# Giving the values' PSUM bank back between runs of products, with the sums gathered in SBUF, and a new written order

## The chip, the cores and the metric

The kernel runs on one core of one Trainium2 chip. The metric is device time of one execution, in microseconds (us). Before the change it is 1624.57 us, the median of three runs (1624.36 to 1624.93). Five engines work side by side, each through its own list of instructions in a fixed order: TensorE (PE in the profile, with its weight loads as PEld), VectorE (DVE), ScalarE (ACT), GpSimd (POOL) and SyncE (SP), which here issues every DMA.

## The reference

All inputs are fp32. `x` is 2048 tokens by 512; attention has 32 heads of 16, and one shared key head and value head.

```
q = (x @ wq) as 32 heads of 16;  k = x @ wk;  v = x @ wv          # k, v: 2048 x 16
p = softmax(q k^T / 4)                                            # per head, 2048 x 2048
a = concat(p @ v) @ wo
b = (sigmoid(x @ w_gate) * (x @ w_up)) @ w_down                   # 512 -> 1792 -> 512
g = sigmoid(sum(x * gate_w))                                      # one number per token
out = g * a + (1 - g) * b
```

The factors on `wq` and `wk` make the scores large, so each row's maximum is taken before the exponential.

## The kernel before, in words

**Units of attention.** The tokens are cut in 4 blocks of 512 and the heads in 8 groups of 4. One block with one group is a unit `u`; there are 32. A unit needs three kinds of products on PE:

- `m` (line 1074): scores with the queries as rows. DVE reduces each 128x512 tile to its row maxima (line 1076). 64 tiles per unit.
- `s` (line 1083): the scores again, turned, with the maxima subtracted by extra rows of the product. ACT takes the exponential of each tile into an SBUF buffer `p` (line 1085). 64 tiles per unit.
- `V` (line 965, function `pv`): the values. One `V` takes the four `p` tiles of one chunk of 128 keys and multiplies them by `v_aug`, in which a row of ones makes the denominators too. A unit has 16 of them, and all 16 add into one PSUM bank; the four matmuls of a `V` go to four groups of 32 rows of that bank.

When a unit's sixteenth `V` is done, ACT copies the bank to the SBUF tile `ou` (line 973, `finish`), five DMAs take it on (lines 981 and 984), and the division and the output projection follow.

**The rest of PE's work** is `f` (line 1053): the matmuls of the gated MLP and of the output projection. Their results leave PSUM through ACT (`gate`, and `part` with "first" or "apart", line 1034) or DVE (`gated`, and `part` with "sum", lines 1063 and 1016). A token tile's first part is written to the tile `ba` by ACT with "first"; later parts are added to it by DVE with "sum", or set apart by ACT and added by GpSimd (line 1037).

**How PE is shared.** The contraction of `m`, `s` and `f` is 64 rows or fewer, so two of them run at a time, one in the upper and one in the lower half of the array. That is one step. A `V` uses all 128 rows, in four groups of 32 columns, so PE changes its tiling before a run of `V`s and again behind it. The first projections (`G` in the order) use the whole array too.

**Banks.** There are 8 PSUM banks. Each `m`, `s` and each group of `f` takes a free one and gives it back when ACT or DVE has read it. The values' bank is held from a unit's first `V` to the copy behind its sixteenth, so that 7 banks are left for the steps.

**What sets the order.** The string `ORDER` is read one character at a time by a planner (`State.step`). `V`, `G` and `T` (a transposition of maxima) stand for themselves; a hexadecimal digit is one step, whose two base-4 digits say what goes into each half (0 nothing, 1 `m`, 2 `s`, 3 `f`); `.` is a short wait. The planner keeps a clock for every engine, a time at which each bank and buffer comes free, and tasks for GpSimd with ranks. It emits the list of actions that the kernel issues, and that list is the fixed order of every engine. The planner's times are not seen by the chip: the engines wait on semaphores.

```
        self.acts.append(("part", h, j, i, "sum"))
        at = self.on("dve", at, SUM)
```

These two lines plan a "sum" on DVE; the time at which ACT has written the tile's "first" does not enter.

Of the kernel before, what the change touches and what calls it, by code (L numbers as in the profile page):

```python
# [18 lines left out]
P = 128  # L19
# [11 lines left out]
RAW, WB, DB, PB, HB, BA_BUFS = 2, 2, 4, 22, 6, 4  # L31
# [18 lines left out]
IN, OUT, VALUES, TURN = 52, 94, 371, 50  # L50
# [60 lines left out]
class State:  # L111

    def __init__(self):
# [3 lines left out]
        self.free, self.sum = [0] * 7 + [4100], None  # L117
        self.later, self.count = [], 0
# [21 lines left out]
        self.held, self.exps = 0, []  # L140
        self.loaded, self.stage_free, self.unit_ready, self.max_ready, self.q_ready = 0, 0, {}, {}, {}
# [60 lines left out]
    def run(self, t):  # L202
        self.tasks.remove(t)
        what, *args = t[3]
        if what == "w":
            wide = args[0][0] in "gu"
            cost = (not self.early(args[0])) * CAST_W + TWO_W if wide else (1 + (args[0][0] != "e")) * (CAST + TWO)
        else:
            cost = {"h": CAST + TWO, "add": TWO, "stack": CAST_W + 2 * TWO_W, "divide": CAST + 2 * TWO, "x": 2 * TWO,
                    "xf": 4 * TWO, "wq": TWO}[what]  # L210
# [60 lines left out]
    def event(self, what, args):  # L271
# [17 lines left out]
        elif what == "store":  # L289
            self.after(self.send(5, 136) + SAFE, "sums", *args)  # L290
# [131 lines left out]
    def gather(self, j, h, i, second, at):  # L422

        key = (j.b, j.i % NT)
        if key not in self.parts:
# [5 lines left out]
            return self.on("act", at, SCALED)  # L431
# [7 lines left out]
        at = self.on("dve", at, SUM)  # L439
# [61 lines left out]
    def can_v(self):  # L501
        return (self.first > GROUPS.index(("turn", NB - 1, 0)) and self.vp < NU * NC and bool(self.exps)
                and (self.vp % NC > 0 or min(self.free) <= self.now)
                and self.exps[0][0] == 4 and self.exps[0][1] <= self.now)

    def issue_v(self):
        u, c = divmod(self.vp, NC)
        if c == 0:
            self.sum = self.take()
        self.acts.append(("values", u, c, self.sum))  # L510
# [5 lines left out]
        if c == NC - 1 and u < NU - 1:  # L516
            self.acts.append(("finish", u, self.sum))
            at = self.on("act", self.now + LATE, COPY) + TAIL_A
            self.free[self.sum] = at + FREE
            self.after(at, "store", u)  # L520
# [76 lines left out]
    def step(self, code):  # L597


        self.tick()  # L600
        if code == ".":
# [25 lines left out]
    "GGGGGGGG555G555G5554GG555G555G55G555GG55G555G555GG555G555GT55.Gd7ffdb6fbdfe7bde7bf9fe7edbf6f9fe7fbde7bfdV696V559"  # L627
    "VVV6bdff79fef7fedb7ff9f6ffdef6fdf6fbdf7bd7VVV9e7ffdb7efdfb7edff6dbff7bf97ffed6ffbd7d.VT69V696V965VV9e7ffdb7efdfb"
    "7edff6f9ff7bf9f7fede7fd7d7VVVb9ef7df6fdbef6fdbf6f9f7bef9fe7fdb6fdbf7ed7V969V696V95aV696Va59V696Va59VT69V569VVe6b"
    "fdfb7ef9fe7bf9f7deVV6bd7ffedbef7bf9f7eef5.V965VVd6bfdb7ef9fe7bdeb7f9fffef6fdbf6f9fe7bdef7V969VVV6fbdef6fbdbf6fd7"  # L630
    "dVVV6fbdbf6fbf9fef6fbdef5f7d7VVVTbb7fffdef97fefedbf6ff9fe7bf9fe7ef9fe7d36V969VV696V596VV96fbfd7bf9fe7edbe7f9f7eb"
    "def7bdef6fdbb7efd7dVVV695VV6bbdff6fbdef6fbdbf6fbd7f9VVVTee7fffd6bfdfbef5V69bfff6fbdef6fbdbf5feVV6bbfdfe7bf9fe7ef"
    "9f7deV695VV6958VV79fe7edbf6fbde7bf9f6ffffedb7ef9f6fdb7edf7VV95aV696V596VV9eb7ff9fe7ef9fe7bf9fe7df6fdbVVVTeb7fffd"
    "6beff.9VV6f9ff7edbf7fedb7ff97effdef6fdfb79ff7edbV55aVV696V969V69fef7dbf6fbd7ef9ef7bf9f6fdeb7efdbf6f9f7d7eVVV969V"
    "696V969V696V9T6Vbe9ff7ef9fe7bf9fe7ef9f7d7VVV9ee7ff9fe7bf5febdV695VV6bedff6fbdbf6fd7df6VVd6bfdb7bf9fe7edbf6f9f7de"
    "bVV696Vb9fe7fed7f9VV6bf9ffe7ebdV69efff6fdb7Vb9ef7fed7f9VVTebefff7b5fefbefd7d7VVb9ef7fedbf6fbdef7d7d7VVbedbf7ef9f"
# [45 lines left out]
def tile_kernel(ctx, tc, x_in, wq, wkv, wo, wg, wu, wd, consts_in, out):  # L682
# [279 lines left out]
    def pv(u, c, ps):  # L962

        for j in range(4):
            nc.tensor.matmul(ps[32 * j:32 * j + 32, :], v_aug[:, c, :], PT.pop((u, c, j)),  # L965
                             start=c == 0, stop=c == NC - 1)

    SUMS = {}
# [213 lines left out]
```

## Time and profile before

| | |
|---|---|
| median of 3 runs | 1624.57 us (1624.36 to 1624.93) |
| profiled execution, its own time | 1625.31 us |
| its span, first to last instruction | 1623.5 us |
| PE busy | 1614.7 us (99%) |
| DVE busy | 1419.7 us (87%) |
| ACT busy | 1187.6 us (73%) |
| POOL busy | 773.8 us (48%) |
| mean clock granted to TensorE | 0.999 of full speed |

In the profile, a row names a line of the kernel, the engine, the operation, and the tiles as output<-inputs, with the number of instructions behind an x. Times are in us unless marked ns. A `V` shows as eight records of line 965, since each of its four fp32 matmuls leaves two. Matmuls are pipelined, so one record (about 0.4 us for a step's matmul) is longer than the distance to the next start; the distance between starts is what a matmul costs.

### The profile page before, as it was taken

What the parts mean: (1) busy time and instruction counts of PE and PEld (TensorE: products, weight loads), DVE (VectorE), ACT (ScalarE), POOL (GpSimd) and SP (SyncE); (2) the same over time, 40 slices, a digit from 0 to 9 for tenths busy, and PEclk for the clock granted to TensorE, in tenths of its full rate; (3) what the DMA queues carried; (4) which work ended last, traced back from release to release, by engine and by line L of the source; (5) the groups of instructions that cost most, each with busy time, mean ns of one, the idle gap of its engine ahead of it and who ended that gap; (6) DMA issues with size and microseconds to landing.
All of it is one profiled execution on the core that took longest, in us unless ns stands there. A gap on an engine that the chain in (4) does not pass through costs nothing.

```text
span 1623.5 us, 33536 instructions
## 1 busy us (share of the span) xinstructions
PE 1614.7 (99%) x12950; PEld 982.2 (60%) x12950; DVE 1419.7 (87%) x2422; ACT 1187.6 (73%) x2274; POOL 773.8 (48%) x598
## 2 busy tenths in 40 slices
PE   9999999999999999999999999999999999999998
PEld 7665566555666566655656556565566656566554
DVE  6999898999998989999998998888998999889842
ACT  4277777677777767777776877767877777777786
POOL 5344264457454534463726346435645454536152
PEclk9999999999999999999999999999999999999999
DMA  7311111024111211111412121102411121111011
GB/s 234 135 52 44 44 54 48 27 71 107 59 45 45 77 35 59 39 44 54 122 32 70 38 76 54 47 29 70 106 60 48 44 76 43 58 31 34 32 35 40
DMA packets 52371, 98.10 MB, mean 60 GB/s; under 512 B 17976, under 2 KB 19512, under 8 KB 51188
## 3 DMA queue, kind: packets, MB, share of 16 engines
q1 hardware_dynamic: 52212, 95.96, 19.2%
q8 instruction: 102, 1.67, 0.4%
q14 instruction: 57, 0.47, 0.1%
HBM read 74.05 MB, written 8.90 MB: 51 GB/s over the span
## 4 chain that ended last, share of the span: by engine, by line
PE 98%; ACT 1%; DVE 1%; DMA 0%; SPq 0%; issue 0%; DVEq 0%; ACTq 0%
PE bank L1053 31%; PE bank L965 30%; PE bank L1074 17%; PE bank L1083 16%; PE bank L819 3%; ACT p L1085 1%; DVE mx L1076 0%; DMA xf<-x_in 0%; PE bank L950 0%; DVE ba L1130 0%; DMA qs<-mt 0%; ACT x L737 0%; PE bank L889 0%; DVE ba L1016 0%; ACT ba L1034 0%
## 5 line engine op out<-in xcount | busy, mean ns | idle before, releaser
L1076 DVE TENSOR_REDUCE mx<-bank 128x1 f32<-128x512 f32 x2048 | 1285.7, 683 | 124.4 <-PE bank L1074 68.4
L1085 ACT ACTIVATE p<-bank 128x512 f32<-128x512 f32 x2048 | 1068.3, 621 | 334.8 <-PE bank L1083 162.2
L1083 PE MATMUL bank<-qs,ks 64*128 64x512 f32 x2048 | 748.4, 408 | 0.4 <-DVE ba L1016 0.3
L1074 PE MATMUL bank<-ks,qs 62*128 62x512 f32 x2048 | 709.7, 410 | 0.6 <-ACT q L911 0.3
L965 PE MATMUL bank<-p,v_aug 128*32 128x512 f32 x4096 | 502.3, 599 | 0.0
L1083 PEld LDWEIGHTS bank<-qs,ks 64*128 64x128 f32 x2048 | 356.4, 185 | 142.0 <-DVE mx L1076 54.7
L1074 PEld LDWEIGHTS bank<-ks,qs 62*128 62x128 f32 x2048 | 341.1, 184 | 160.1 <-DVE mx L1076 68.2
L1053 PE MATMUL bank<-wd,hl 64*128 64x512 f32 x1344 | 261.4, 394 | 0.0
L965 PEld LDWEIGHTS bank<-p,v_aug 128*32 128x32 f32 x4096 | 102.7, 108 | 226.8 <-issue 208.6
L1053 PE MATMUL bank<-xs,wg 64*128 64x512 f32 x672 | 210.6, 393 | 0.0
L1053 PE MATMUL bank<-x,wu 64*128 64x512 f32 x672 | 209.6, 392 | 0.0
L1053 PE MATMUL bank<-xs,wu 64*128 64x512 f32 x672 | 209.1, 393 | 0.0
L1053 PE MATMUL bank<-x,wg 64*128 64x512 f32 x672 | 206.8, 392 | 0.0
L1053 PEld LDWEIGHTS bank<-wd,hl 64*128 64x128 f32 x1344 | 182.0, 185 | 29.7 <-DVE mx L1076 6.7
L937 POOL TENSOR_TENSOR qs<-stage,qs 16x1024 fp32r<-16x1024 f32 x62 | 148.8, 2400 | 4.8
L1053 PEld LDWEIGHTS bank<-x,wu 64*128 64x128 f32 x672 | 118.3, 185 | 10.2 <-DVE mx L1076 0.8
L1053 PEld LDWEIGHTS bank<-xs,wu 64*128 64x128 f32 x672 | 117.4, 186 | 10.3 <-issue 2.5
L1053 PEld LDWEIGHTS bank<-xs,wg 64*128 64x128 f32 x672 | 118.4, 186 | 7.3
L1053 PEld LDWEIGHTS bank<-x,wg 64*128 64x128 f32 x672 | 116.9, 186 | 8.5 <-POOL wu L795 0.8
L794 POOL CAST wu<-ru 128x1024 fp32r<-128x1024 f32 x27 | 28.0, 1038 | 175.7 <-PE bank L1053 140.5
L1037 POOL TENSOR_TENSOR ba<-ba,pa_d 128x512 f32<-128x512 f32 x48 | 61.8, 1290 | 76.0 <-DVE ba L1016 46.1
L935 POOL CAST qs<-stage 128x1024 fp32r<-128x1024 f32 x31 | 32.2, 1039 | 131.2 <-PE bank L1083 90.6
(85 smaller groups left out, 1074.0 us busy)
## 6 DMA issues: line engine op xcount, KB each, us to landing
rg<-wg SPq DMA_DIRECT2D x28, 512.0 KB
ru<-wu SPq DMA_DIRECT2D x28, 512.0 KB
rd<-wd SPq DMA_DIRECT2D x28, 512.0 KB
stage<-qd SPq DMA_DIRECT2D x192, 64.0 KB
xs<-x SPq DMA_DIRECT2D x16, 512.0 KB
xf<-x_in SPq DMA_DIRECT2D x16, 256.0 KB
qd<-q SPq DMA_DIRECT2D x16, 256.0 KB
ra<-wo SPq DMA_DIRECT2D x8, 512.0 KB
```

The lines of the kernel that those rows point to most:

```text
L794: nc.gpsimd.tensor_copy(WS[item][:, 0, :], raw)
L819: nc.tensor.matmul(ps, w[:, p, part(kc)], X[b, kc][:, q, :], start=i == 0, stop=i == 3 * KC - 1)
L935: (nc.scalar.copy if u == 0 else e.tensor_copy)(qs, stage)
L937: e.tensor_tensor(qs[r], stage[r], f32(qs[r]), op=ALU.subtract)
L965: nc.tensor.matmul(ps[32 * j:32 * j + 32, :], v_aug[:, c, :], PT.pop((u, c, j)), start=c == 0, stop=c == NC - 1)
L1037: nc.gpsimd.tensor_tensor(BA[b, t], BA[b, t], PA.pop((b, t)), op=ALU.add)
L1053: nc.tensor.matmul(banks[i], l, r, start=at == 0, stop=at == j.n - 1)
L1074: nc.tensor.matmul(banks[i], qs_t[u % 3][r, pr, part(qt)], ks[r, kb * 512:(kb + 1) * 512], start=True, stop=True)
L1076: nc.vector.tensor_reduce(MX[u][:, pr, h, qt, kb:kb + 1], banks[i], axis=AX.X, op=ALU.max)
L1083: nc.tensor.matmul(banks[i], ks[r, part(c)], qs_t[u % 3][r, pr, :], start=True, stop=True)
L1085: nc.scalar.activation(p, banks[i], AF.Exp, scale=0.25)
```

## The change

1. **The bank is given back between runs.** A new character `C` in the order closes the values' bank: the `V` ahead of it ends its accumulation there, ACT copies the sums so far to one of two SBUF tiles (`sums_out`, which replaces `finish`), and the bank is free again. The next `V` takes a new bank and starts it afresh. The first closing of a unit leaves its sums in a tile `OU[n]`; each later one is copied to the other tile, and GpSimd adds it on (`sum_add`, a 128x512 fp32 addition, a task of rank 1). Behind the unit's last closing the sums are stored from `OU[n]`. The last unit is not closed; the kernel's end reads its bank as before.
2. **One `p` buffer fewer** (PB from 22 to 21), for the second `ou` tile.
3. **The planner's book-keeping:** a "sum" is planned no earlier than its tile's "first" (`first_at`), and a `T` counts 20 in place of 50 of the planner's units.
4. **A new order string.** Counted in both strings, with `C` left out of the count of runs:

| | before | after |
|---|---|---|
| `V` | 512 | 512 |
| `G`, `T` | 24, 32 | 24, 32 |
| steps (hexadecimal digits) | 4265 | 4259 |
| of these with one half empty | 30 | 18 |
| `.` | 10 | 13 |
| `C` | 0 | 99 |
| runs of `V` | 303 | 251 |
| runs of one, two, three `V` | 146, 105, 52 | 60, 121, 70 |
| runs of `G` followed by a step or `T` | 14 | 12 |

The numbers of `m`, `s` and `f` are the same in both (2048, 2048 and 4404). With the 31 units that are closed at their end there are 130 closings, where 31 copies were.

```diff
-RAW, WB, DB, PB, HB, BA_BUFS = 2, 2, 4, 22, 6, 4
+RAW, WB, DB, PB, HB, BA_BUFS = 2, 2, 4, 21, 6, 4
-IN, OUT, VALUES, TURN = 52, 94, 371, 50
+IN, OUT, VALUES, TURN = 52, 94, 371, 20
...
+        elif what == "sum_add":
+            u, i, n, last = args
+            self.ou_free[i] = at
+            if last:
+                self.after(at, "store", u, n)
...
-            return self.on("act", at, SCALED)
+            self.first_at[key] = self.on("act", at, SCALED)
+            return self.first_at[key]
...
-        at = self.on("dve", at, SUM)
+        at = self.on("dve", max(at, self.first_at[key]), SUM)
...
-        if c == 0:
+        new = self.sum is None
+        if new:
             self.sum = self.take()
...
+    def close(self, u, last):
+        self.acts[self.v_at] = (*self.acts[self.v_at][:4], True, self.sum)
+        i = self.ou_free.index(min(self.ou_free))
+        assert self.ou_free[i] <= self.now or last
+        self.acts.append(("sums_out", i, self.sum))
+        at = self.on("act", max(self.now + LATE, self.ou_free[i]), COPY) + TAIL_A
+        self.free[self.sum], self.sum, self.ou_free[i] = at + FREE, None, NEVER
+        if self.ou is not None:
+            self.task(1, at + SURE, "sum_add", u, i, self.ou, last)
+        elif last:
+            self.after(at, "store", u, i)
+        else:
+            self.ou = i
+        if last:
+            self.ou = None
...
+        if code == "C":
+            self.close(self.vp // NC, False)
...
-    def pv(u, c, ps):
+    def pv(u, c, new, last, ps):
...
-                             start=c == 0, stop=c == NC - 1)
+                             start=new, stop=last)
...
-        SUMS[u] = ap.tile([P, TB], F32, tag="ou", name=f"ou{u}", bufs=1)
-        nc.scalar.copy(SUMS[u], ps)
+    OU = [ap.tile([P, TB], F32, tag=f"ou{i}", name=f"ou{i}", bufs=1) for i in range(2)]
+    def sums_out(i, ps):
+        nc.scalar.copy(OU[i], ps)
+    def sum_add(_, i, n, last):
+        nc.gpsimd.tensor_tensor(OU[n], OU[n], OU[i], op=ALU.add)
```

More of the change, by code (lines that the diff above doesn't have):

```diff
@@ L208, in run @@
         else:
-            cost = {"h": CAST + TWO, "add": TWO, "stack": CAST_W + 2 * TWO_W, "divide": CAST + 2 * TWO, "x": 2 * TWO,
+            cost = {"h": CAST + TWO, "add": TWO, "sum_add": TWO, "stack": CAST_W + 2 * TWO_W, "divide": CAST + 2 * TWO, "x": 2 * TWO,
                     "xf": 4 * TWO, "wq": TWO}[what]
@@ L289, in event @@
         elif what == "store":
-            self.after(self.send(5, 136) + SAFE, "sums", *args)
+            u, i = args
+            self.ou_free[i] = self.send(5, 136)
+            self.after(self.ou_free[i] + SAFE, "sums", u)
         elif what == "sums":
@@ L502, in can_v @@
         return (self.first > GROUPS.index(("turn", NB - 1, 0)) and self.vp < NU * NC and bool(self.exps)
-                and (self.vp % NC > 0 or min(self.free) <= self.now)
+                and (self.sum is not None or min(self.free) <= self.now)
                 and self.exps[0][0] == 4 and self.exps[0][1] <= self.now)
@@ L507, in issue_v @@
         u, c = divmod(self.vp, NC)
-        if c == 0:
+        new = self.sum is None
+        if new:
             self.sum = self.take()
-        self.acts.append(("values", u, c, self.sum))
+        self.v_at = len(self.acts)
+        self.acts.append(("values", u, c, new, c == NC - 1, self.sum))
         self.now += VALUES
@@ L516, in issue_v @@
         if c == NC - 1 and u < NU - 1:
[L517 to L520, printed above, removed]
+            self.close(u, True)
+    def close(self, u, last):
[13 more added lines that the diff above has]
+            self.ou = None
     def can_t(self):
@@ L597, in step @@
     def step(self, code):
-        self.tick()
-        if code == ".":
+        if self.last != "C":
+            self.tick()
+        if code == "C":
+            self.close(self.vp // NC, False)
+        elif code == ".":
             self.now += 25
@@ L632 @@
[L632 to L636, printed above, removed]
@@ new lines @@
+    "ef9f6fbdef6f9fb7d7df5fVVV65VVC97edfbf6ff96fbdf6fbdef6f9fb7edbf6fbde7fbd7dVVC655VV965VVCb9f6ffde7bf9fTffee6ffdb7b"
+    "f9f6f9f6fdeb7efd7.VVV965VV9e6ffdf6fbdbf6f9fb7ed7bedbf7edbf6fdbe7bfd7dV696VVC965VVC97fedb7ef9fe7bdef6f9f7VVVC97fe"
+    "db7ef9fe7bdef6f9f7VVCTbf9fff79fe7edef6ff97VVC97defb7ef9f6fbde7bf5feVV965VV97f9fe7fedb7ef9f7ef9fe7bdef6f9fb7ef9f6"
+    "fbde7VV955VVVC6d7bfedbf6f9fe7dbef6ff9f6fbdb7ef9fe7bdef5f7VV9TaVVVC69fef7dbf6fbf97ef9f6fdeb7efdb7ef9f7ebd7fd7dVVV"
+    "696V965VV9e6ffdf6fbdb7dbe7bfdef6f9f7bedbf7ef9f6fd7d7VV969V696VCd6bbfd7ef9fe7bdef6f9fbVVC6T9VVVC69fef7dbf6fbde7bf"
@@ new lines @@
+    "9f6fdVVC69fef7dbf6fbde7bf9f6fdV696VV965VVd6bfdb7ef9fe7bdef6f9f7VVC9e6ffdf6fbdbf6f9f6f9fb7edbf7edbf6fbde7bfd7dVVV"
+    "696V596VVCTfbff9ff69f6ff9fe7edbf6f9fe7bf9f6fedf6fbd7.V969V696V95aV6a5VV969VV56fbfedbf6f9fe7bdef6fbdb7efdb7ef9fe7"
+    "bd7f5fdVVV696V9a6V969VVC6fdbf6fbdef6db7bf9f7eedbf7edbfTff6fbdff6d7VVV96aV596VVC96fdfb7ef9f6fbde7fb9fe7f9fe7edfb6"
+    "fdbfe7d7d7VVVdb6ff9fe7bdV696VV96aV969VC6fdbf6f9fe7ffbfdef7fbfed6fbd7..VV9TaVC6bdef7bdfe7bedb7d7fedbVVVC6bdef7f9f"
+    "e7bedb7def7dbVVC6bdef7bdfe79feb7d7fedbVVV6bdef7bdfe7bedb7edf6f1bVVVC6bdbf7edfbf6dfbf6bdfe79f7ef9ef7bf9f7edf6fdV6"
@@ new lines @@
+    "96V965VV9T5VVC69fbf7def6fbd7bedbf7ef9f6fdbe7bfdef6f9f7bdVV69eV569VVVC6dfb7bdef6f9f7bedbf7ef9f6fdbe7bfdef6f9f7d7d"
+    "VV696VV969VVC6dbf7bdef6fbdb7edbf6ff9e7bfdefb7edbfTff6fdVV695VVVC65ffbfdbe7bdfe7bdef6fbdb7ef9f6fbdef7bdef7dVV696V"
+    "C5bf9fe7bf9f6fedb7dfebVVV79fefef6f9fbe7dbf6f9feVVV695VVC69fbf7edfb7edbf6f9fe7fbff9ff6f9fe7ef9fe7dVVV6T9V695VVC6d"
+    "fb7bdef6fbdb7ef9f6ffffbf9f6fedbf6f9f7deVVV696VV9ff6db7bf9fe7ebdff69feVVC6bdbf7edfb7ebde7d7fbdeVVVC6bdbf7edfbf6bf"
+    "9ef6fdf6f9f7bf9f7f9eef7fde7dVVV6T9VVC6fdbf6f9f6f9f7bedbf7ef9f6fdbe7bfdef6f9f7d7dVV69aV655VVVdb6fbdb7ff96fedff6bd"
@@ new lines @@
+    "bf7edbf6f9fe7bf9f6fed7dVVVCa65VVC9f7bde7bf9fe7edb7ef9fe7dbef7bf9fe7edbfTff5cV695VVC6df6fbdbf6f9fe7bdef5fbVVVC65f"
+    "bfedbf6f9fe7bdef7beVVV969VV7edbf6f9fe7bfde7bf9f7fef9f7eef9f7ef9f6fdbV696V965VVV965VVC9f7ef9fe7bfTefbdef79e7bfdef"
+    "6f9fb7edbf6fbd7dVVV696VVC95ffeb7efdb7ef9f6fbdef6f9fb7edbf7ef9f6fbd7dVVV696VV969VCe797fef9feb7def6f9f7bef9f7ef9f6"
+    "fbdef6f5fd7VVV96bV596VVCTbebffdf6dbf6fbde7dfbe6ffdbf6f9fb7edbf6fd7VVCa95VV696VVC96fbfd7ef9fe7bdeb7f9fe7ebdf7edbf"
+    "6fdbe7bfd7dVVV6bf9ff6fd7dVV6b9fff6fdebVVC6bdf7ef9fe7ffbed7fbdV696VVCTb9fff7f9ee7fdef6fdbbVVC6db7fedbf6f9fe7bdef6"
@@ new lines @@
+    "fbVVC97edfbe7f9f6fbde7bfde7V955VVV7e5fbfdeb7f9fe7edbff6VVC95fefb7ef9f6fbde7fb9fe7f9fe7edbf6fbdef7d7d7VV969VVVCTe"
+    "6fffdf6b9ff7bdef6fbdb7ef9f6fbdef6fdbf7bdVV696V969V696VVVC9e7bfff9f6efd6fbdb7ef9f6fbdfe7bdef6f5fdbbfVV655VVVC97fe"
+    "db7ef9f6fbde7bf9fe7edbf7edbf6fbde7bfd7dVVV6T9V696VVC96bffd7ef9fe7bdef6f9f7bedbf7edbf6fdbe7bfd7dVVVC65bffedbf6f9f"
+    "e7bdef6fbVVVC95effb7ef9f6fbde7bf9feVVV695VVC6dbef7dbf6fbf97eedf6fffbf9f7ef9f6fbde7bfeVVV969VT69VVC69fef7dbf6fbde"
+    "7bf9f6feVVC96fbfd7ef9f6fbde7bf9feVVC6bdef7dbf6f9fe7bdef5fbVV69fef7dbf6f9fe7bdef6fbVVV965VVC97fdef7bf9ef7ef9f6fbd"
@@ new lines @@
+    "e7bf9fe7edbf6fdbf6fd7VVV969V6T9VVC6f97fedbf6f9fe7bdef6fbdb7efdb7efdbe7bdfe7d7VVV965VV5b9ffe7ef9f6fbdf6bf9ff6f9f7"
+    "eedbf7ef9f6fbd7dVVVC695VVC6bedfb7df6fbdef6f9fb7edbf6ff9f6fbde7bfd7d7d..VVV6T5VVC97edfb7ef9f6fbf97ef9feVVC65bffed"
+    "bfe79fe7bdef7beVVC96fdfb7efbd6fbde7bf9feVV6f97fedbf6f9fe7bdef7bdVV695VVC696VVC96fdfbfe79f6fdbef6fdbf6fdfb6bfdf6f"
+    "bdbf6fd7VVV9T6VVC96fdfb7ef9f7ebde7fbdef6f9fb7debf6ff9f6fbd7dVVV695VV7e9f7dfe7bedf7bedbf7ef9f6fdbe7bfdef6f9f7bdVV"
+    "V695VVC6bedfb7df6fbdef6f5fbbedfff6bdbf7edbf6fbd7dVVV6T9V696VVC97dfeb7efdb7ef9f6fbdef6f9fb7edbf7ef9f6fbd7dVVV696V"
@@ new lines @@
+    "969V6db7fdebf6fV969Ve6bdffb7ef9V696VCd6bdfb7ef9fffe7d7fbeVVVC96bffdf6f9f6fbdef6fbdbVV6T9VVC6fdbf6f9fe7bf9f6fedb7"
+    "fffef97ef9f6fdbe7bfdVVV695VV5e6ffbdbf6f9fe7bdef6fbVVC9e7bfdf6fbdef6f9f6f9f7db7efdf6fbdff6f9ff7V969V569VVCa55VVCT"
+    "f6fdfbf6bdf7ebdef7bf9f6fdeb7efdbf6f9f7ebdVVV695VVC69fef7dbf6f9f7ebdef7bf9f6fdeb7efdbf6f9f7d7dVV696VV969V696VVC9f"
+    "7ef9f6fbdef6f9fb7ebdf6d7fbdfe7befdb7efbdVV6T5VVVC95effbf6fbdef6f9fb7d7ebfefd6f9fb7ef9fe7bd7dVV696VV96aV596VV5b9f"
+    "fe7ef9f6fbde7bf9feVVC6fdbf6f9fe7bf9f6fedb7dVVVC6fdbf6f9fe7bf9f6fedb7ffdebf7ef9f6fbd7fed7VVV9T6V969V696VCb9f7efde"
@@ new lines @@
+    "7bf9fe7ed6fd7b.VVVC9ef6fdfb7bf97edefb7ed7VV9e7bfdf6fbdef6f97bfd7eVVVC9ef6fd7bf9fe7bdef6f9fbVVVC6bf9f7def6fbde7bf"
+    "9f6fedbf6fdbf6fbdef6f9f7d7VVVT95VVC69ff7edbf6f9fe7bf9f6fedb7efdbf6f9fe7bdef5f7VV965VVVd6bfdb7ef9f6fbde7bf9fe7edb"
+    "f7edbf6fbde7bf5fdVVV696V969VVC6fdbe7bdfeb7edb7f9f7eedbf7edbfTff6fbdff6d7VVC969VVC6d7bfedbf6f9fe7bdef6fbVVVC96bff"
+    "d7ef9f6fbde7bf9feVVC6f97fef9f6f9fe7bdef5f7VV965VVC97edfb7ef9f6fbde7bf9feVV696VVC96fdfbf6f9f6fbdef6fdbbfTff6fdbf6"
+    "bfdef6f9f7VVV965VVC9f6fbdf6fbdef6f97bf9fe7edbf7edbf6fbde7bfd7dVVV696VV965VCbde7fbde7bf9f6fedbf6f9fe7bdfe7bf9f6fe"
@@ L671 @@
+    "db7dfVV69aV565VVVCTbeffd7f9eb7ff9f6fedb7ef9fe7bdef6f9ff6fbd7VV96aV596VVVC9f5efb7ef9f6ffdb6bfdfe7bdef6f9fb7ef9f6f"
+    "bd7d.VVV69aVV6bdeff6fbbdVVC6f9fe7dfbefff7bdebe7VVC9fe7db7efbe.9.VV6bf9ffefefTbffebfebVVVebeffbefbfefbfefb.VVebef"
+    "bfefbfefbffebVVVebeffbeffbeffffb2.82VVaaVbefbVebebfVeafbffffefbebfffeVVbefbfebfeffbeVVbefbfebfeffbeVVaaVeec8V8ee"
+    "ccV88cccccV"
 )
@@ L960, in tile_kernel, with store @@
     PT, VD, OT = {}, {}, {}
-    def pv(u, c, ps):
+    def pv(u, c, new, last, ps):
         for j in range(4):
             nc.tensor.matmul(ps[32 * j:32 * j + 32, :], v_aug[:, c, :], PT.pop((u, c, j)),
-                             start=c == 0, stop=c == NC - 1)
+                             start=new, stop=last)
+    OU = [ap.tile([P, TB], F32, tag=f"ou{i}", name=f"ou{i}", bufs=1) for i in range(2)]
     SUMS = {}
-    def finish(u, ps):
-        SUMS[u] = ap.tile([P, TB], F32, tag="ou", name=f"ou{u}", bufs=1)
-        nc.scalar.copy(SUMS[u], ps)
-    def store(u):
+    def sums_out(i, ps):
+        nc.scalar.copy(OU[i], ps)
+    def sum_add(_, i, n, last):
+        nc.gpsimd.tensor_tensor(OU[n], OU[n], OU[i], op=ALU.add)
+    def store(u, i):
         if u % 2 == 0:
@@ L1094, in tile_kernel @@
         "m": maximum, "max_finish": max_finish, "max_turn": max_turn, "send_max": send_max, "s": scores,
-        "values": on_bank(pv), "finish": on_bank(finish), "store": store, "sums": sums, "invert": invert, "send_inverse": send_inverse,
+        "values": on_bank(pv), "sums_out": on_bank(sums_out), "sum_add": sum_add, "store": store, "sums": sums, "invert": invert, "send_inverse": send_inverse,
         "spread": spread, "divide": divide,
```

44 lines of the change are left out of this document (4 added, 40 removed).

## The prediction, made before the run

> **What bounds the kernel now.** I read the page's busy times and its chain of work first, to see which engine sets the end.
>
> ```profile
> span 1623.5 us, 33536 instructions
> PE 1614.7 (99%) x12950; PEld 982.2 (60%) x12950; DVE 1419.7 (87%) x2422; ACT 1187.6 (73%) x2274; POOL 773.8 (48%) x598
> PE 98%; ACT 1%; DVE 1%; DMA 0%; SPq 0%; issue 0%; DVEq 0%; ACTq 0%
> ```
>
> The chain that ends last lies on PE for 98% of the span. Two readings are possible: PE has that much to do, or it waits inside matmuls that only look busy. The view of who waited for whom, for PE alone (the longest of seven rows) and for the weight loads of `m`, comes next.
>
> ```profile
> PE bank L841 <- POOL v_aug L835: 1.3, 1, 1.3
> ```
>
> ```profile
> PEld bank L1074 <- DVE mx L1076: 68.2, 85, 0.8
> ```
>
> Matmuls hardly wait. The weight loads' 68.2 us "for DVE" are 85 pieces of 0.8 us in the mean and 0.8 at most, as alike as a fixed price and not as a queue; so DVE may be only the last signal seen, and the place must say what they are. The timeline of PE over a stretch with runs of one, three and two `V` does (start and length in us; 8 records of line 965 are one `V`):
>
> ```profile
> 1110.14 1.06 PE L965 MATMUL bank<-p,v_aug 128*32 128x512 f32 x8
> 1111.13 0.49 PE L1083 MATMUL bank<-qs,ks 64*128 64x512 f32 x1
> ...
> 1111.48 0.60 PE L1083 MATMUL bank<-qs,ks 64*128 64x512 f32 x2
> 1111.71 0.39 PE L1074 MATMUL bank<-ks,qs 62*128 62x512 f32 x1
> 1112.03 1.06 PE L965 MATMUL bank<-p,v_aug 128*32 128x512 f32 x8
> ...
> 1115.84 2.78 PE L965 MATMUL bank<-p,v_aug 128*32 128x512 f32 x24
> 1118.55 0.50 PE L1074 MATMUL bank<-ks,qs 62*128 62x512 f32 x1
> ...
> 1119.45 1.92 PE L965 MATMUL bank<-p,v_aug 128*32 128x512 f32 x16
> 1121.30 0.50 PE L1074 MATMUL bank<-ks,qs 62*128 62x512 f32 x1
> ```
>
> From the first `V` to the first step behind it pass 0.99 us for one `V` (1110.14 to 1111.13), 1.85 for two (1119.45 to 1121.30) and 2.71 for three (1115.84 to 1118.55): 0.86 us per `V` and 0.13 us that each run pays once. The first step then takes 0.35 us to the second (1111.13 to 1111.48), the second 0.23, and the last step before a `V` 0.32 (1111.71 to 1112.03). The price of a step in a long stretch comes from the next two rows, which are 40 steps apart:
>
> ```profile
> 1239.79 0.39 PE L1083 MATMUL bank<-qs,ks 64*128 64x512 f32 x1
> ...
> 1249.11 0.40 PE L1053 MATMUL bank<-xs,wg 64*128 64x512 f32 x1
> ```
>
> That is 9.32 / 40 = 0.233 us. From one single-`V` run to the next in the rows above 1.89 us pass (1110.14 to 1112.03) for one `V` and three steps: 1.89 - 0.86 - 3 x 0.233 = **0.33 us for one change of tiling there and back**, the same whatever the label of the wait is. So the order's own counts should rebuild the time. The row of the values' weight loads gives first and last start:
>
> ```profile
> L965 PEld LDWEIGHTS bank<-p,v_aug x4096: 106/109/110, 88.5 to 1613.0; 128*32 128x32 f32 x196
> ```
>
> Between first and last `V` (1524.5 us) the old order has 4187 steps (78 of the 4265 stand ahead), 511 `V` and 302 boundaries: 4187 x 0.233 + 511 x 0.86 + 302 x 0.33 = 975.6 + 439.5 + 99.7 = 1514.8 us. All that is left for transpositions, short waits and stalls is 9.7 us, 0.6%. The kernel is bounded by the number of characters in its order, and by how often it changes between steps and `V`.
>
> **The change, part by part.**
>
> *Fewer boundaries.* Runs of `V` go from 303 to 251 and runs of `G` from 14 to 12, so 54 changes of tiling there and back are gone. That a boundary beside `G` costs the same is taken over from `V`; it is 2 of the 54. 54 x 0.33 = **17.8 us off**. The bounds of this term: 0.33 less the 0.1 by which the first step is long (if that part were a wait for ACT or DVE) gives 54 x 0.23 = 12.4; if all of the 9.7 us left above belonged to the 302 boundaries, each would cost 0.33 + 0.03, and the term is 19.4. I take 0.33, since it holds in every run shown.
>
> *Fewer steps.* 6 x 0.233 = **1.4 us off**. Three more short waits cost 3 x 0.06 = 0.2 us (a `.` counts 25 in the code that counts a step 100). The `V`, `m`, `s` and `f` are as many as before.
>
> *A "sum" planned behind its "first".* The timeline shows a "sum" that stood for its "first", and the row of the group what that made in all:
>
> ```profile
> 177.64 0.75 DVE L1016 SCALAR_TENSOR_TENSOR ba<-bank,gom,ba 128x512 f32<-128x512 f32 x1 [1.16 <-ACT ba L1034]
> ```
>
> ```profile
> L1016 DVE SCALAR_TENSOR_TENSOR ba<-bank,gom,ba 128x512 f32<-128x512 f32 x64 | 47.5, 743 | 18.4 <-PE bank L1053 10.1 <-PE bank L1083 5.2 <-ACT ba L1034 3.0
> ```
>
> DVE stands 1.16 us for ACT there. In the whole span DVE waits 3.0 us for this; PE's loss lies between 0 and 3.0. I take **1.5 us off**, because the wait reaches PE only where banks have run out.
>
> *Copies on ACT.* 99 more of this kind (0.587 us, 58.1 us in all; ACT's busy share goes to 78%):
>
> ```profile
> L973 ACT COPY ou<-bank 128x512 f32<-128x512 f32 x31 | 18.2, 587 | 39.5 <-PE bank L965 39.5
> ```
>
> ```profile
> 1290.67 0.50 PE L1074 MATMUL bank<-ks,qs 62*128 62x512 f32 x1
> ...
> 1290.81 0.59 ACT L973 COPY ou<-bank 128x512 f32<-128x512 f32 x1 [1.24 <-PE bank L965]
> ...
> 1291.01 0.39 PE L1083 MATMUL bank<-qs,ks 64*128 64x512 f32 x1
> ...
> 1291.47 1.58 ACT L1085 ACTIVATE p<-bank 128x512 f32<-128x512 f32 x3
> ```
>
> ```profile
> 406.13 0.49 PE L1083 MATMUL bank<-qs,ks 64*128 64x512 f32 x1
> ...
> 406.66 0.60 ACT L1085 ACTIVATE p<-bank 128x512 f32<-128x512 f32 x1 [1.78 <-PE bank L1053]
> ```
>
> No `s` comes during a run of `V`, so ACT has run dry (it stood 1.24 us) when the copy comes, 0.14 us after PE's first step. The copy ends 0.73 us after that step, and the exponential begins 0.80 after it (1291.47). Without a copy the first exponential begins 0.53 us after its `s` (406.13 to 406.66). Here the first `s` is in the second step (1291.01) and its exponential could not have begun before 1291.54: no delay. Where the first step holds an `s`, the delay is 0.80 - 0.53 = 0.27. The cover is the hole that the run leaves. At most 99 x 0.27 = 26.7 us of ACT, into an idle share of 22%. On PE's path I take **0**; with the cover gone it is 26.7. If a copy is late, the bank comes back late and the exponentials behind it.
>
> *Additions on GpSimd.* 99 of 1.29 us (by the row of its other fp32 addition of that size) are 127.7 us; POOL goes from 774 to 901 us of work, 56%.
>
> ```profile
> L1037 POOL TENSOR_TENSOR ba<-ba,pa_d 128x512 f32<-128x512 f32 x48 | 61.8, 1290 | 76.0 <-DVE ba L1016 46.1 <-ACT pa_d L1034 18.9 <-ACT p L1085 9.8
> L795 POOL TENSOR_TENSOR wg<-rg,wg 128x1024 fp32r<-128x1024 f32 x28 | 66.9, 2389 | 7.1 <-ACT wg L785 5.0
> ```
>
> Behind an addition that waits for its copy stand the splits of weights and of the gated tiles, which `f` waits for; they have room, as POOL is idle for the other 44%. Could the additions slow DVE? First a stretch in which POOL stood idle for 25.09 us up to 176.15, with DVE's reductions inside it, then one in which POOL was at work:
>
> ```profile
> 176.15 1.04 POOL L935 CAST qs<-stage 128x1024 fp32r<-128x1024 f32 x1 [25.09 <-PE bank L1053]
> ```
>
> ```profile
> 161.41 3.66 DVE L1076 TENSOR_REDUCE mx<-bank 128x1 f32<-128x512 f32 x6
> ```
>
> ```profile
> 1142.05 4.88 POOL L937 TENSOR_TENSOR qs<-stage,qs 16x1024 fp32r<-16x1024 f32 x2
> ```
>
> ```profile
> 1144.56 3.08 DVE L1076 TENSOR_REDUCE mx<-bank 128x1 f32<-128x512 f32 x5 [0.62 <-PE bank L1074]
> ```
>
> Six reductions in 3.66 us and five in 3.08 are 0.61 and 0.62 each: no difference, so 0. The Trainium skill (SBUF — State Buffer, Who interferes with whom) has a rule that speaks against more work on GpSimd: VectorE and GpSimd share a pair of ports under an exclusive lock, and a VectorE instruction with two SBUF inputs waits out a GpSimd instruction that reads SBUF. Were DVE's work of that kind, the sum would be worse by up to 127.7 us, 1732; the same section exempts instructions with at most one SBUF input, and the rows above show the exemption to hold here.
>
> *The bank, the `p` buffer, the store.* That 8 banks serve the steps between runs, and that one `p` buffer is gone, has its effect through which characters the order could hold; both are in the counts. The five DMAs of a unit stay five, one addition later.
>
> *Sum.* 17.8 + 1.4 + 1.5 - 0.2 = 20.5. For stalls that the new order has and no row of the old can show I take off 0.5, a part of the 9.7 us that was unexplained before: **20 us** off. The span of 1623.5 becomes 1603.5; the execution that was profiled took 1625.31, within 0.05% of the median, so from the median 1624.57 follows **1604.6 us**.
>
> **Rivals.**
>
> *Late sums (slower).* ACT may not copy into an `ou` tile before GpSimd has read it, and every exponential behind the copy waits too. In the new string 12 of the 130 closings follow the one before by less than 4.5 us (by the prices above). If GpSimd is then busy with a weight split of 2.39 us and its own 1.29, one late closing costs up to 3.68 us; six undo the gain. All twelve: 1604.6 + 44.2 = 1648.8. For it: in-order queues, and POOL does stand for 25 us at times. Against: two tiles take turns, and it is idle 44% of the time.
>
> *Half the gain (DVE).* DVE is busy 87% and will be 88.5%. If the reductions cannot be packed closer, steps wait for their banks and DVE gives back half: 1614.6. Against: by the rows above it takes 0.61 us per reduction, 2048 x 0.61 = 1249 us.
>
> *No change.* The 0.33 us could be a wait in disguise (for the exponentials that a `V` needs), which fewer, longer runs would only gather: 1604.6 + 17.8 = 1622.4. Against: it is the same behind one, two and three `V`.
>
> **How the numbers follow.** Forecast 0.74, with its own range of 1600 to 1611.5: below, 19.4 in place of 17.8, 3.0 in place of 1.5 and no new stalls give 1601, and I leave one us more; above, 12.4 in place of 17.8 and nothing for the "first" give 1611.5. Half the gain 0.13, no change 0.07, late sums 0.06. The range 1600 to 1614.6 holds the forecast and the nearer side of half the gain, about 0.8. About 0.2%, 3.2 us, is what a measurement can tell from no change: faster 0.87, same 0.07, slower 0.06.
>
> **What would show it.** Right: the steps still 0.233 us apart, 0.86 us per `V`, 0.33 per boundary; PE's own waits still under 5 us; no wait of DVE line 1016 for ACT's "first"; DVE, ACT and POOL busy 1420, 1246 and 901 us in a span near 1603. Wrong: ACT's copies waiting for POOL, or PE's weight loads waiting over 0.84 us at many places behind a closing.

## The result, and the profile after

The new kernel takes **1603.92 us** (median of four runs, 1603.85 to 1606.78; before on the same chip 1624.46). The ratio is 0.9878 with a 95% interval of 0.986 to 0.9895: 20.5 us less. The forecast was 1604.6 us and 20 us less. In a second series, beside an old kernel of 1624.81 us, it took 1603.27 us, 21.5 less.

The page of the new kernel, its busy times and the shares of the chain that ended last:

```profile
span 1605.0 us, 33714 instructions
PE 1593.3 (99%) x12950; PEld 988.5 (62%) x12950; DVE 1389.3 (87%) x2422; ACT 1221.5 (76%) x2373; POOL 897.6 (56%) x697
...
PE 97%; POOL 1%; DMA 1%; SPq 0%; issue 0%; ACT 0%; DVE 0%; DVEq 0%; ACTq 0%; POOLq 0%
```

PE is as full as before, with the same 12950 records in 18.5 us less of span. (The profiled execution is the slowest of the four, 1606.78 us.) POOL has its 99 additions, ACT its 99 copies. The chain has a new guest: 1% POOL and 1% DMA. The view of what PE waited for names the place:

```profile
PE bank L1109 <- ACT ou L1004: 2.1, 1, 2.1
PE bank L872 <- POOL v_aug L866: 1.3, 1, 1.3
```

There is one wait of 2.1 us, for a copy of the sums. It is followed below, in the part on rank 0.

The timeline of PE around a run of two `V` in the new kernel (line 996 is the old line 965, 1109 the `m`, 1118 the `s`), and the row of the values' weight loads:

```profile
800.32 0.39 PE L1118 MATMUL bank<-qs,ks 64*128 64x512 f32 x1
800.64 1.92 PE L996 MATMUL bank<-p,v_aug 128*32 128x512 f32 x16
802.50 0.49 PE L1118 MATMUL bank<-qs,ks 64*128 64x512 f32 x1
```

```profile
L996 PEld LDWEIGHTS bank<-p,v_aug x4096: 106/110/110, 93.9 to 1592.6; 128*32 128x32 f32 x196
```

Two `V` still take 1.86 us to the next step, and 0.32 pass between the last step and the `V`. So the old prices may be put on the new counts: from first to last `V` there are 4151 steps (108 stand ahead), 511 `V` and 250 boundaries, 967.2 + 439.5 + 82.5 = 1489.2 us. The row gives 1592.6 - 93.9 = 1498.7. The rest is 9.5 us, where the old order left 9.7. This execution was the slowest of its four; a second trace of the same kernel (an execution of 1603.06 us) has this row:

```profile
L996 PEld LDWEIGHTS bank<-p,v_aug x4096: 106/110/110, 93.7 to 1590.5; 128*32 128x32 f32 x196
```

That is 1496.8 us, and 7.6 are left. The difference arises at the wait shown above, where the second trace is 2.0 us shorter. The new time is the old list of prices on a shorter list of work.

### The profile page after: what moved, and what is told of

The parts are those of the page before. It is cut to its first block, busy times and chain, and to the rows that moved or that the text cites. A ratio compares the mean times of both kernels' runs of the same rounds, so it can differ in the third digit from the quotient of the medians.

```text
span 1605.0 us, 33714 instructions
## 1 busy us (share of the span) xinstructions
PE 1593.3 (99%) x12950; PEld 988.5 (62%) x12950; DVE 1389.3 (87%) x2422; ACT 1221.5 (76%) x2373; POOL 897.6 (56%) x697
## 4 chain that ended last, share of the span: by engine, by line
PE 97%; POOL 1%; DMA 1%; SPq 0%; issue 0%; ACT 0%; DVE 0%; DVEq 0%; ACTq 0%; POOLq 0%
PE bank L1088 31%; PE bank L996 29%; PE bank L1109 17%; PE bank L1118 16%; PE bank L850 3%; DMA vd<-ou 0%; DMA wqr<-wq 0%; POOL x L785 0%; POOL qs L968 0%; PE bank L981 0%; SPq L1019 0%; SPq L1016 0%; DVE ba L1165 0%; POOL ba L1072 0%; SPq L753 0%
## 5 line engine op out<-in xcount | busy, mean ns | idle before, releaser
L1111 DVE TENSOR_REDUCE mx<-bank 128x1 f32<-128x512 f32 x2048 | 1256.4, 679 | 138.4 <-PE bank L1109 76.8
L1120 ACT ACTIVATE p<-bank 128x512 f32<-128x512 f32 x2048 | 1056.1, 623 | 177.7 <-PE bank L1118 89.2
L1118 PE MATMUL bank<-qs,ks 64*128 64x512 f32 x2048 | 758.0, 405 | 0.0
L996 PE MATMUL bank<-p,v_aug 128*32 128x512 f32 x4096 | 491.4, 598 | 0.0
L1118 PEld LDWEIGHTS bank<-qs,ks 64*128 64x128 f32 x2048 | 363.6, 185 | 122.0 <-DVE mx L1111 41.1
L1088 PE MATMUL bank<-x,wu 64*128 64x512 f32 x672 | 217.3, 393 | 0.0
L1088 PE MATMUL bank<-xs,wu 64*128 64x512 f32 x672 | 216.7, 392 | 0.0
L1088 PE MATMUL bank<-x,wg 64*128 64x512 f32 x672 | 214.3, 392 | 0.0
L1007 POOL TENSOR_TENSOR ou<-ou,ou 128x512 f32<-128x512 f32 x99 | 127.8, 1291 | 124.6 <-ACT ou L1004 112.2
L1004 ACT COPY ou<-bank 128x512 f32<-128x512 f32 x130 | 76.4, 588 | 145.4 <-PE bank L996 74.1
```

The costliest lines, as they stand in the source:

```text
L1004: nc.scalar.copy(OU[i], ps)
L1007: nc.gpsimd.tensor_tensor(OU[n], OU[n], OU[i], op=ALU.add)
L1088: nc.tensor.matmul(banks[i], l, r, start=at == 0, stop=at == j.n - 1)
L1111: nc.vector.tensor_reduce(MX[u][:, pr, h, qt, kb:kb + 1], banks[i], axis=AX.X, op=ALU.max)
L1118: nc.tensor.matmul(banks[i], ks[r, part(c)], qs_t[u % 3][r, pr, :], start=True, stop=True)
L1120: nc.scalar.activation(p, banks[i], AF.Exp, scale=0.25)
```

## The experiments

All times are medians; "the new kernel" is 1603.3 to 1603.9 us, the medians of two series of runs.

### What a boundary costs: 54 and 108 put back

```diff
 ORDER (at 54, or 108, places)
-  ...VVd...     a run of two or three V, then a step
+  ...VdV...     the last V behind that step; a C stays behind the last V
```

> The new kernel with 54 boundaries put back: at 54 places a V changes places with the step behind it (VVx becomes VxV). 305 runs of V in place of 251; V, steps, closings and short waits are as many as in the new kernel. Theory (a change of tiling costs PE 0.33 us wherever it stands): 1603.9 + 54 x 0.33 = 1621.7 us, within 2. Rival (the 0.33 is a wait for exponentials in disguise, which only moves): 1604 to 1607 us.

> The same with 108 boundaries put back (359 runs of V). Theory: 1603.9 + 108 x 0.33 = 1639.5 us, twice the step of the run with 54. Rival (a wait in disguise): 1604 to 1610 us, and not twice the other.

Measured: **1620.87 us** with 54 (ratio to before 0.9974, 0.9965 to 0.9983) and **1637.01** with 108 (1.0075, 1.006 to 1.009). Against 1603.27 for the new kernel, run later beside an equal old kernel (1624.81 and 1624.84), that is 17.6 and 33.7 us: 0.33 and 0.31 us per boundary. The price is nearly the same for both, it adds up, and it is not a wait that moves elsewhere. 54 boundaries are most of the gain.

### The new order without giving the bank back

```diff
 ORDER
-  (99 C)
+  (none; where a bank or its user is not ready by the plan, short waits are written in: 1342 in place of 13)
```

A written wait is no instruction on the chip; it only moves the planner's clock. The `V` and the steps come in the new sequence.

> The new order without its 99 closings inside a unit: the values' bank is held from a unit's first V to its sixteenth as in the old kernel, 31 copies, no additions; the order of V and steps is the new one. Theory (the bank given back is what makes that order possible): PE stands for banks, and the time is above the old kernel's 1624.5 us. Rival (the new order alone makes the gain, the bank is not needed): 1602 to 1606 us.

Measured: **1658.49 us** (ratio 1.0207, 1.019 to 1.0225), 54.6 us above the new kernel and 34 above the old. The order by itself is a loss; with 7 banks it cannot run as written. (The planner's clock also places GpSimd's tasks and the DMAs, so these may have moved with the written waits.) The waits of PE's matmuls do not show the loss (the longest is 1.3 us, for `v_aug` at the start). The weight loads do. Here is what they waited for on ACT's exponentials and DVE's reductions, first in the new kernel, then without the bank given back (line 1099 is `f` there, 1120 `m`, 1129 `s`):

```profile
PEld bank L1109 <- DVE mx L1111: 45.0, 57, 0.8
PEld bank L1118 <- DVE mx L1111: 41.1, 51, 0.8
...
PEld bank L1109 <- ACT p L1120: 14.8, 24, 0.8
PEld bank L1118 <- ACT p L1120: 11.6, 32, 0.8
```

```profile
PEld bank L1129 <- DVE mx L1122: 58.3, 112, 0.8
PEld bank L1120 <- DVE mx L1122: 53.6, 96, 0.8
PEld bank L1120 <- ACT p L1131: 38.5, 155, 0.8
...
PEld bank L1129 <- ACT p L1131: 26.3, 112, 0.8
```

These waits rise from 112.5 to 176.7 us, and those for ACT from 56 to 267 in number. Nearly all of the loss lies in the long stretches of steps: compared from `V` to `V` with the second trace of the new kernel, 53.8 us fall into 80 of the 511 distances, 0.4 to 1.2 us in each. The timeline shows what happens there. First the new kernel in such a stretch, where both halves of a step start within 0.01 us:

```profile
803.06 0.39 PE L1088 MATMUL bank<-x,wg 64*128 64x512 f32 x1
803.07 0.39 PE L1088 MATMUL bank<-xs,wg 64*128 64x512 f32 x1
803.30 0.39 PE L1088 MATMUL bank<-x,wg 64*128 64x512 f32 x1
803.31 0.39 PE L1118 MATMUL bank<-qs,ks 64*128 64x512 f32 x1
```

Then the new order without the bank given back:

```profile
1110.71 0.39 PE L1099 MATMUL bank<-xs,wg 64*128 64x512 f32 x1
1110.77 0.40 PE L1099 MATMUL bank<-x,wg 64*128 64x512 f32 x1
1110.94 0.39 PE L1120 MATMUL bank<-ks,qs 62*128 62x512 f32 x1
1111.01 0.45 PE L1129 MATMUL bank<-qs,ks 64*128 64x512 f32 x1
1111.18 0.39 PE L1099 MATMUL bank<-x,wg 64*128 64x512 f32 x1
1111.29 0.40 PE L1099 MATMUL bank<-xs,wg 64*128 64x512 f32 x1
```

The halves have come apart by 0.06 to 0.11 us. From 1111.01 to 1111.29 one half takes 0.28 us for its step, while the other keeps to 0.23 to 0.24, so PE never looks idle. That such a matmul waits for its bank is read from the weight loads' waits and not from these rows.

### Copies and additions alone, in the old order

```diff
-    for what, *args in plan():
+    todo = plan()
...
+    for n, (what, *args) in enumerate(todo):
         acts[what](*args)
...
+        if n in ends:                    # 99 ends of runs of V inside a unit
+            more = ap.tile([P, TB], F32, tag="ou", name=f"more{n}", bufs=1)
+            nc.scalar.copy(more, banks[end])
+            nc.gpsimd.tensor_tensor(more, more, more, op=ALU.add)     # not in the second kernel
```

The `V` behind such a copy starts the same bank afresh.

> The old order with 99 more copies by ACT and 99 more additions by GpSimd behind runs of V, and nothing gained by them: the bank is not given back to the steps. The sums ahead of such a copy are lost (the next V starts the bank afresh; the addition doubles the copied tile), so the output is not the reference's. Theory (copies hide in the hole that a run of V leaves on ACT, additions in GpSimd's idle time): 1624 to 1628 us. Rival (each copy's 0.27 us of delay reaches PE): 1624.5 + 26.7 = 1651 us.

Measured: **1642.77 us**, 17.9 above the old kernel (ratio 1.0109, 1.0094 to 1.0124). That lies between the two numbers that were expected. The waits for the `ou` tile, and the place of the longest on POOL and on ACT:

```profile
ACT ou L975 <- POOL more L1113: 16.0, 5, 5.5
...
PE bank L1076 <- ACT ou L975: 5.1, 1, 5.1
...
PE bank L1085 <- ACT ou L975: 3.4, 2, 2.3
```

```profile
329.22 4.79 POOL L937 TENSOR_TENSOR qs<-stage,qs 16x1024 fp32r<-16x1024 f32 x2
334.09 1.04 POOL L1113 TENSOR_TENSOR more<-more 128x512 f32<-128x512 f32 x1
```

```profile
335.16 0.58 ACT L975 COPY ou<-bank 128x512 f32<-128x512 f32 x1 [5.49 <-POOL more L1113]
```

This is the rival "late sums" of the prediction: the addition stands behind two splits of 2.4 us on GpSimd, ACT stands 5.49 us for the tile, and PE 5.1 us for ACT. Three such places make 5.1 + 3.4 = 8.5 us. I put the other 9 down to the copies and left the additions out:

> The old order with the 99 more copies by ACT, without the 99 additions. Sums ahead of a copy are lost, so the output is not the reference's. With copies and additions the old order took 17.9 us more than without, of which the profile shows 8.4 us at three places where ACT waited for the one ou tile, in the additions' hands. Theory (the rest is the copies, in an order that was not planned around them): 1624.8 + 9 = 1634 us, within 3. Rival (it was the additions and the tile alone): 1625 to 1627 us. Rival (the copies alone make all of it): 1642 us.

Measured: **1627.56 us**, 2.75 above the old kernel measured beside it (ratio 1.0016, 1.0007 to 1.0025): **0.03 us per copy**. My theory fell. The copies are almost free; the additions and the one tile made 15 of the 17.9 us. The profile shows 8.5 of the 15 as waits of PE, but the starts of the `V` in the two traces show more. They are the same `V` in both; first with the additions, then without:

```profile
328.32 1.07 PE L967 MATMUL bank<-p,v_aug 128*32 128x512 f32 x8
...
347.28 1.06 PE L967 MATMUL bank<-p,v_aug 128*32 128x512 f32 x8
```

```profile
326.63 1.06 PE L967 MATMUL bank<-p,v_aug 128*32 128x512 f32 x8
...
337.84 1.06 PE L967 MATMUL bank<-p,v_aug 128*32 128x512 f32 x8
```

This stretch, with the copy that stood 5.49 us, takes 18.96 us in place of 11.21. The stretches of two other copies that stood for an addition (4.05 and 3.67 us) are longer by 4.1 and 1.6 us. So 13.5 of the 15 us lie at three late tiles. POOL's own standing, 330.9 us for ACT's copies over the whole span, made little of the loss.

### The additions left out, and given to DVE

```diff
     def sum_add(_, i, n, last):
-        nc.gpsimd.tensor_tensor(OU[n], OU[n], OU[i], op=ALU.add)
+        pass                                                          # first kernel
+        nc.vector.tensor_tensor(OU[n], OU[n], OU[i], op=ALU.add)      # second kernel
```

> The new kernel with GpSimd's 99 additions left out, so that the sums of a unit's later closings are lost and the output is not the reference's; all copies, stores and the order stay. GpSimd has 127.8 us less to do, and no copy can wait for an addition. Theory (the additions lie in GpSimd's idle time): 1601 to 1604 us. Rival (additions hold PE up through late tiles or ports): faster by more than 5 us, under 1599.

Measured: **1603.65 us** (ratio 0.9869, 0.9855 to 0.9884), the new kernel's time. In the new order, where the planner has a place for each addition, GpSimd's 127.8 us cost nothing, although POOL stands 112 us for ACT's copies there too.

> The new kernel with the 99 additions on DVE in place of GpSimd, at the same places of the list: by the row of its 128x512 subtraction of two SBUF tiles (853 ns in the old profile) 84 us more work for DVE, about 1474 us, 92%. It measures DVE's slack. Theory (PE's list is the time, DVE has room): 1604 to 1615 us. Rival (DVE is nearly the bound, and gave back a part of the gain already): most of the 84 us shows, above 1640 us.

Measured: **1653.76 us** (ratio 1.0177, 1.016 to 1.0194), some 50 us more. That is the rival's side. The rows of the additions on DVE and of what PE then waits for:

```profile
L1007 DVE TENSOR_TENSOR ou<-ou,ou x99: 669/680/2848, 114.9 to 1604.0; 128x512 f32<-128x512 f32 x99
```

```profile
PE bank L1109 <- DVE mx L1111: 6.9, 16, 1.8
PE bank L1118 <- DVE mx L1111: 3.4, 9, 1.0
```

81.3 us of additions (822 ns in the mean) cost PE 50: DVE has little slack at these places, though it was busy 87% only. Most of it shows in the weight loads again, whose waits for DVE's reductions at lines 1109 and 1118 rise from 86.1 to 134.0 us. The additions take 680 ns in the median and up to 2848. The Trainium skill (SBUF — State Buffer, Who interferes with whom) says that a VectorE instruction with two SBUF inputs contends with a GpSimd instruction that reads SBUF; the spread from 680 to 2848 ns agrees with that, while the reductions (one input, from PSUM) kept 679 ns with the additions on either engine. The longest addition, and GpSimd's work beside it:

```profile
414.10 2.85 DVE L1007 TENSOR_TENSOR ou<-ou,ou 128x512 f32<-128x512 f32 x1
```

```profile
414.02 2.37 POOL L826 TENSOR_TENSOR wu<-ru,wu 128x1024 fp32r<-128x1024 f32 x1
```

It began 0.08 us into the weight split and ended 0.55 us behind it. So did all 21 that took 700 ns or more: each began while a GpSimd instruction was at work and ended 0.54 to 0.55 us behind its end. Additions that were under way when GpSimd's instruction began kept their 680 ns.

### How much cover the copies have

```diff
     def sums_out(i, ps):
-        nc.scalar.copy(OU[i], ps)
+        for _ in range(2):
+            nc.scalar.copy(OU[i], ps)
```

> The new kernel with each of its 130 copies by ACT made twice (the same bank to the same tile), so that the bank comes free 0.49 to 0.59 us later and every exponential behind stands as long: 130 x 0.587 = 76 us more work for ACT (1298 us of some 1604, 81%). It asks how much cover the copies have left. Theory (the hole of a run ends with the first copy, but ACT idles a fifth of its time and the steps have 8 banks): a small part reaches PE, 1606 to 1625 us. Rival (ACT is the pace behind each run): 1603.9 + 130 x 0.5 = 1669 us. Rival (cover is ample): 1604 us.

Measured: **1650.11 us** (ratio 1.0154, 1.0139 to 1.0169), 46 us more for 130 copies, 0.36 each in the mean, between the theory and the rival. From `V` to `V` against the second trace of the new kernel, nearly the whole loss lies behind the closings: 0.4 to 0.6 us behind 79 of the 130, less behind 27, and 0.1 or nothing behind 24. The first copy costs 0.03 where the bank stays reserved; the second, in an order with no room for it, most of its 0.62 us at most places. Behind most closings the hole is about as long as one copy.

### The late tile: additions at rank 0

The wait of 2.1 us above, followed back in the new kernel's timeline (POOL, then SP, then ACT):

```profile
1133.05 4.74 POOL L785 TENSOR_TENSOR x<-rx,x 128x1024 fp32r<-128x1024 f32 x2
1137.73 1.32 POOL L1007 TENSOR_TENSOR ou<-ou,ou 128x512 f32<-128x512 f32 x1
```

```profile
1138.69 1.99 SPq L792 DMA_DIRECT2D xs<-x  x1
1140.72 0.60 SPq L793 DMA_DIRECT2D xs<-x  x1
1141.42 2.43 SPq L1016 DMA_DIRECT2D sd<-ou  x1
1143.90 3.51 SPq L1019 DMA_DIRECT2D vd<-ou  x4
```

```profile
1152.63 0.58 ACT L1004 COPY ou<-bank 128x512 f32<-128x512 f32 x1 [4.25 <-DMA vd<-ou]
```

The unit's last addition lies behind two splits of `x` (4.74 us), its five DMAs behind the transfers of `xs`, and ACT stands 4.25 us until the last has read the tile. The kernel without the additions keeps this wait (4.1 us, at the same store), so it is the store's place behind the `xs` transfers that counts, and not GpSimd's 1.3 us.

```diff
-            self.task(1, at + SURE, "sum_add", u, i, self.ou, last)
+            self.task(0, at + SURE, "sum_add", u, i, self.ou, last)
 ORDER: one short wait more, the rest as in the new kernel
```

> The new kernel with the planner's rank of a sum's addition changed from 1 to 0, so that GpSimd takes it ahead of splits of x and additions of parts that are waiting (the written order gets one short wait more). In the profiled execution of the new kernel ACT stood 4.25 us for an ou tile: its last addition lay behind two splits of x on GpSimd, its store behind the transfers of x on SP. Theory (that one late tile is what the profiled execution of 1606.8 us had over the others of 1603.9): no wait of ACT's copy for that store in the profile, 1602 to 1604 us. Rival (the additions now hold up the splits that f waits for): 1606 us or more.

Measured: **1602.22 us** (ratio 0.9859, 0.9845 to 0.9874). The same chain in a second run of this version:

```profile
1133.05 1.27 POOL L1007 TENSOR_TENSOR ou<-ou,ou 128x512 f32<-128x512 f32 x1
1134.29 4.74 POOL L785 TENSOR_TENSOR x<-rx,x 128x1024 fp32r<-128x1024 f32 x2
```

```profile
1149.67 0.59 ACT L1004 COPY ou<-bank 128x512 f32<-128x512 f32 x1 [1.35 <-PE bank L996]
```

The addition goes first, its store ahead of the `xs` transfers (1134.35 on SP's queue), and the copy comes 2.96 us earlier and waits for PE alone. Both versions on one chip:

> The new kernel unchanged, beside the version with rank 0 on the same chip. 1603 to 1605 us; in the profile ACT waits once for the store of an ou tile, 1 to 5 us, near 1150 us of the span.

> The version with the additions at rank 0 once more, on the same chip as the new kernel. Theory (the late store costs the new kernel 1 to 2 us in most executions, not in the profiled one alone): 1.5 to 2 us under the new kernel of this call. Rival (the 1.7 us between them was the chip): within 0.5 us of it.

Measured: **1603.27 us** (1603.06 to 1603.66) for the new kernel, with ACT's wait of 3.5 us for the store at the same place, and **1602.33** (1601.97 to 1602.52) with rank 0; against the old kernel 0.9865 (0.985 to 0.988) and 0.9859 (0.9842 to 0.9875). The two sets of times don't meet, and the medians lie 0.94 us apart: less than the 1.5 us I gave it, more than the rival's 0.5. In the traces of these two the difference lies at this place: PE's step behind the wait starts at 1152.43 us in the new kernel and at 1150.81 with rank 0. So the late store is in the new kernel's ordinary time, at 1 to 2 us, and rank 0 is the fastest version here.

### The "first" in the old kernel, with four places of its order rewritten

```diff
-            return self.on("act", at, SCALED)
+            self.first_at[key] = self.on("act", at, SCALED)
+            return self.first_at[key]
...
-        at = self.on("dve", at, SUM)
+        at = self.on("dve", max(at, self.first_at[key]), SUM)
 ORDER: other sequences of the same kinds of codes at four places (V 27 to 33, 158 to 165, 286 to 291, 414 to 421), five short waits more
```

> The old kernel with one part of the change alone: its planner asks when a tile's first part is done before it plans a sum (first_at), and about 280 characters of the old order, at the four places where that matters, are put in another sequence. V, steps, runs (303) and copies are as many as before; five short waits more. Theory (the term of 1.5 us): 1624.8 - 1.5 = 1623.3 us, between 1622.3 and 1624.0, and DVE's longest wait for ACT's first part falls under 1.0 us. Rival (those waits cost PE nothing): 1624.8 us.

Measured: **1621.64 us**, 3.35 less than the old kernel (ratio 0.9979, 0.997 to 0.9989). The waits of DVE's sums for ACT's first parts, old and mended:

```profile
DVE ba L1016 <- ACT ba L1034: 3.0, 5, 1.2
```

```profile
DVE ba L1018 <- ACT ba L1036: 0.8, 1, 0.8
```

The run does not measure the "first" alone, since about 280 characters came in another sequence. By the starts of the `V` in one trace of each, PE gains 3.0 us at the four places together. At three of them the wait is gone, 2.3 us in all, and PE gains 2.2. At the second (`V` 158 to 165) DVE still stands 0.75 us, as it did before, and PE gains 0.8 all the same, from the other sequence. So where the wait went, PE gained about as much, and not half of it; why, was not shown.

## Why the prediction was right, point by point

- **The bound.** Right. The prices of a step, of a `V` and of a boundary leave 9.5 us of the new kernel's 1498.7 unexplained (7.6 in its second trace), as they left 9.7 of the old.
- **Fewer boundaries, 17.8 us.** Right. Boundaries put back cost 0.31 to 0.33 us each, which makes 16.7 to 17.8 for 54. "No change" (a wait in disguise) is excluded by both runs. The 2 of the 54 that stand beside `G` were not tested by themselves.
- **Fewer steps, 1.4 us.** Not measured by itself; the rebuilt sum contains it.
- **The "first", 1.5 us.** Not settled. The old kernel with the "first" mended gains 3.35 us (1.8 to 4.9 us), above the upper bound of 3.0 as a median, but part of that is its other sequence. Where the wait went, PE gained the whole of it and not half. In the new kernel five such waits are left, 2.3 us in all (four and 1.9 in its second trace), so DVE's 3.0 us fell by 0.7 to 1.1 only. The reason given, that the wait reaches PE only where banks have run out, was not tested.
- **Copies on ACT, 0 with a bound of 26.7.** Nearly right: 99 copies in the old order cost 2.75 us. But the cover is thin, as the rows said; a second copy costs 0.36 in the mean.
- **Additions on GpSimd, 0.** Right in the new order, where leaving them out changes nothing. The ground given, 44% of idle time, was too weak: in the old order, whose plan had no place for them, the additions and the shared tile cost 15 us, nearly all of it at three copies that came late.
- **New stalls, 0.5 us.** The late store is 1 to 2 us. The mechanism is that of the rival "late sums", at one place; what held the tile there was the store's DMAs and not the addition itself.
- **Half the gain (DVE).** It did not come, but the argument against it (2048 x 0.61 = 1249 us) was no argument: the new kernel's DVE could not take 81 us more without giving up 50. The new order as planned fits into DVE; work at places that the plan had not kept free does not.
- **What would show it.** DVE's busy time fell to 1389 us where 1420 was expected, with the same 2048 reductions at 679 in place of 683 ns. The records overlap (2048 x 0.679 is 1391 us, and the row of the reductions has 1256 us busy), so busy time is no fixed sum of work. ACT's was 1222 us where 1246 was expected, POOL's 898 where it was 901. PE's own waits, 4.3 us in all, stayed under 5. The waits of sums for "firsts" are fewer microseconds (2.3), not none; none is over 0.7 us.

By the measured terms, 16.7 to 17.8 + 1.4 + 3.35 - 0.2 - 1 gives 20.3 to 21.4 us; with 0.7 for the "first", by which DVE's waits fell, it gives 17.6 to 18.7. Measured were 20.5 and 21.5. Which of the two holds in the new kernel is not shown. The large term was right by its mechanism. That the forecast came within 0.5 us is partly luck: the gain of the "first" and the loss by the late store were sized before any run had shown either, and an error in the one can offset an error in the other.

## What to carry to other kernels

Where one engine is full, price its work from the distances between starts, count how often each price is paid, and rebuild the old time before you forecast the new one: if the sum closes, the change is worth what its counts say. Idle shares do not tell whether added work is free; its place in an in-order list does, and what else waits for the buffer that it holds. In an order with a place for them, 99 additions of 1.29 us were free; in one without, and with a single tile, 99 of 1.04 us cost 15 us.

## What was not expected of the hardware

Two halves of PE that run different matmuls can slip against each other. With banks short, their starts lay 0.06 to 0.11 us apart in the stretch shown, in place of 0.01, and 54.6 us were lost that no wait of PE's matmuls shows. The weight loads' waits show them, 64 us more.

The change of tiling there and back, 0.31 to 0.33 us, appears in the waits of the weight loads as pieces of 0.8 us lost to whichever signal came last before them, most often DVE's reductions. The price was the same, within 6%, for 54 boundaries put back and for 108, and these pieces behind a run of `V` go from 222 in the new kernel to 268 and 311.

An addition of two SBUF tiles on DVE that began while GpSimd was at work ended 0.54 to 0.55 us behind GpSimd's instruction, however long that was, in all 21 cases of 700 ns or more: the longest took 2848 ns in place of 680.
